# Banded attention with a feed-forward layer: q and k of tile 2 transposed by DMA at one visit of three, score runs joined, one gelu and a table load moved, half of a value load moved

## The chip, the cores and the metric

The kernel runs on one core of one Trainium2 chip. The metric is the time of one execution in device microseconds; the profile shows one execution with its engines TensorE (PE, with its weight loads as PEld), VectorE (DVE), ScalarE (ACT), GpSimd (POOL) and SyncE (SP).

## What is computed

Sliding-window attention over 8 batches of 8 heads, 576 positions, head dimension 64, followed by a two-layer feed-forward over all 4608 tokens of width 512 (hidden width 2048). The reference, cut to what matters:

```python
scores = q @ k.T / sqrt(64)
scores = where(abs(i - j) <= 32, scores, -1e9)
attn   = softmax(scores)
x      = (attn @ v)            # heads side by side: 4608 x 512
h      = x @ w_in
out    = (h * sigmoid(1.702 * h)) @ w_out
```

Inputs and output are float32 in device memory.

## The kernel before, in words

**Units and tiles.** The tokens are cut into 36 *units* of 128 (`NU`) and 9 *tiles* of 512, four units each (`NT`). A unit's attention needs its own 128 keys and the 64 after them. For each unit:

- POOL issues DMAs that load q, k and v with a conversion to bfloat16 (`load_kq`, L137; `load_v`, L208; both together in `fetch`, L802, or by choice in `ahead`, L794). q and k land in staging buffers, five of each (L140). v lands in one of nine tiles `ve`; POOL then copies the odd half-blocks into `vo` (`odd_v`, L218).
- q and k are transposed to `qT` and `kT`, either by DMA from SP's queue (`T_dma`, L236; `turn`, L811, is the pair q u, k u+1) or by TensorE (`T_pe`, L242: four 128x128 transposes for each operand into PSUM, then one copy for each on ACT). Both write a buffer given by `place` (L231).
- `scores` (L267) makes 24 matmuls on 64x64 tiles of the array into two PSUM banks, and two exponentials on ACT that write `p`. `band` (L308) multiplies `p` by the window's mask on VectorE. `values` (L316) makes 32 matmuls on 128x64 tiles, with a column of ones for the softmax sum. `norm` (L335) divides on VectorE. `x_T` and `x_T2` (L385, L400) transpose the result for the feed-forward; in the steady tiles the DMA does it from SP's queue (L393).
- The pairs (0, 1) and (2, 3) run through `scores_pair` (L286), 40 matmuls for two units, since five blocks of 64 keys cover two units together.

**Feed-forward.** Tile 0 runs its first layer plainly (`layer1_plain`, L477), either a 512-column matmul for one ff tile of 128 or, with `half`, two ff tiles of 256 columns each; with `later` the gelu is put on a list and run afterwards, and with `kept` VectorE first copies the result out of PSUM. The other tiles use a seven-product scheme for 2x2 blocks in both layers (`l1_group`, L512; `layer2`, L597), whose sums of weights (`w1_sums`, `w2_sums`), of x (`x_sums`, into `xs`) and of g (`g_sums`, `g0_sum`) VectorE forms. In `l1_group`, products 1, 7, 6, 2, 5, 4, 3 follow each other; VectorE adds into `e` (L537) and into `c` (L543), and ACT runs four gelus (L524). Between the products, `fill` puts in matmuls of the second layer, popped one by one from the list `l2`, and sums for VectorE, from the list `dv`.

**What sets the order.** It is written out by hand: every engine executes its instructions in the order in which the Python code issues them. Each DMA queue (POOL's for loads, SP's for stores and DMA transposes) is in order too: an instruction that waits holds back all behind it. A buffer is taken again when what used it is done.

The parts around the change: `opening` (L662) does the attention of units 0 to 7 and the first layer of tile 0; `first_layer1` (L958) does the first layer of tile 1 in four groups n = 0 to 3, loads q, k and v of units 12 to 16 and turns q and k 8 to 14; `run` (L895) then does the attention of units 8 to 15 between second-layer matmuls and hands over to `back(2)` (L847), the first layer of tile 2, and to the steady loop of `front` and `back`.

In `first_layer1` before, for group n:

```python
if n == 3: self.turn(12); self.turn(13)
self.odd_v(8 + n, gpsimd); self.fetch(12 + n)
... at fill 7 of groups 1, 2, 3:
self.T_pe([("k8","q8","k9"), ("q9","k10","q10"), ("k11","q11","k12")][n - 1], scalar)
```

ACT's gelu and its exponential need different function tables; the first use after the other kind stands behind a table load. A one-element exponential on `spark` (L743) sets the place of the load in the opening.

Of the kernel before, what the change touches and what calls it, by code (L numbers as in the profile page):

```python
# [22 lines left out]
SQ = 64  # L23
# [3 lines left out]
class _Kernel:  # L27
# [180 lines left out]
    def load_v(self, u, which=slice(None)):  # L208
# [3 lines left out]
        for off, b, s, n in list(self.pieces(128 * u, 128))[which]:  # L212
            self.nc.gpsimd.dma_start(t[off:off + n, :, :self.D], self.v[b, :, s:s + n, :].rearrange("h s d -> s h d"))  # L213

    def odd(self, u):
        return self.vo[u % 5 if u < 16 else (2, 3, 4, 0)[u % 4]]
# [49 lines left out]

    def scores(self, u, tag):  # L267
# [15 lines left out]
        for eo in range(2):  # L283
            self.nc.scalar.activation(p[:, eo].rearrange("k h s -> k (h s)"), sc[eo], AF.Exp, scale=self.scale)  # L284

    def scores_pair(self, u):  # L286
# [16 lines left out]
        for x in range(2):  # L303
            for eo in range(2):
                self.nc.scalar.activation(p[:, eo, x].rearrange("k h b s -> k (h b s)"), sc[2 * x + eo], AF.Exp,
                                          scale=self.scale)

    def band(self, u, eng=None):  # L308
# [3 lines left out]
        pv = p.rearrange("p e (h b) s -> p (e h) b s", b=2)  # L312
        msk = self.mask[:, a:b + 1:b - a, :].rearrange("p (o b) s -> p o b s", o=1)
        (eng or self.nc.vector).tensor_mul(pv, pv, msk.to_broadcast([128, 8, 2, SQ]))  # L314
# [39 lines left out]
    def values_four(self, u):  # L354
# [5 lines left out]
        for tag in self.FOUR:  # L360
            lo, n, pad = self.four(tag)
            for i in range(n):
                x, h = divmod(lo + i, self.H)
                at, more = pad + i * (D + 1), pad * (i == 0)
                for blk in range(2):
                    vt = (self.ve[(u + x) % 9], self.odd(u + x))[blk].rearrange("p h d -> p (h d)")
                    self.mm(self.acc[u][tag][64 * blk:64 * blk + 64, at - more:at + D + 1],
                            p[x][:, h % 2, h // 2 * 2 + blk, :], vt[:, h * (D + 2) - more:h * (D + 2) + D + 1],
                            start=(i == 0))
# [199 lines left out]
    def layer2_plain(self, t, pr):  # L569
# [3 lines left out]
        def part(i, f):  # L573
# [88 lines left out]
    def opening(self):  # L662
# [80 lines left out]
        act.activation(self.spark, self.spark, AF.Exp)  # L743
        gelus = []
        kept = [self.sb("s7", [128, 512], F32, 2)]
        room = self.sb("xs", [128, 2, 512], F32, 1, "room")
        kept += [room[:, i, :] for i in range(2)]
        h[:], n[0] = ["LA"], 0
        l1(1, 10, later=gelus, kept=kept[0])
        for i in (3, 1):  # L750
# [8 lines left out]
        self.scores(5, "t")  # L759
        l1(None, 12, later=gelus, kept=kept[1])  # L760
        self.scores(6, "BE")
        self.band(4)
        l1(None, 13, later=gelus, kept=kept[2])
        self.scores(7, "AC")
# [130 lines left out]
    def run(self):  # L895
# [20 lines left out]
        do(more, 4)  # L916
        self.values(8, "t")
# [18 lines left out]
        self.scores(14, "BE")  # L936
        do(more, 4)
        self.x_T(10, "A", dve)
        do(more, 2)
        self.x_T(11, "C", dve)  # L940
        self.scores(15, "t")
        do(more, 2)
        do(self.x_sums(2))
        self.seed2 = dve
        self.odd_v(14, pool)
# [12 lines left out]
    def first_layer1(self):  # L958

        def b(*which):  # L960
            return [lambda i=i, j=j: self.w2_sums((i,), j) for i, j in which]

        dv = b((3, 0), (3, 1), (1, 0), (1, 1))
        extra = {0: [lambda: self.w1_sums((4,), 1), lambda: self.g0_sum(1)] + b((2, 0), (2, 1)), 1: b((4, 0), (4, 1)),
                 2: [lambda: self.g0_sum(2)], 3: []}
        for n in range(4):
            if n == 3:
                self.turn(12)
                self.turn(13)
            self.odd_v(8 + n, self.nc.gpsimd)  # L970
            self.fetch(12 + n)

            def fill(i):
                self.do(self.l2, dict(zip((1, 7, 2, 4), ((1, 1, 3, 3), (1, 1, 3, 5), (2, 2, 8, 4), (2, 2, 6, 6))[n]))[i])
                self.do(dv, {1: 2, 7: 1, 2: 0, 4: 2}[i] if n else {1: 0, 7: 1, 2: 0, 4: 1}[i])
# [3 lines left out]
            self.l1_group(1, n, fill, lambda i: self.do(dv, 1))  # L979
            dv += self.g_sums(1, 2 * n, 2) + extra[n]  # L980
        return dv
# [46 lines left out]
```

## Time and profile before

| What | us |
|---|---|
| three runs, median (lowest to highest) | 279.79 (279.43 to 280.37) |
| the profiled execution | 279.59 |
| its span | 277.8 |
| TensorE busy, of the span | 266.3 |
| VectorE, ACT, POOL busy | 212.1, 197.3, 138.6 |

The profile is a page of summaries and a trace that answers questions. A row of a timeline has the start in us from the span's start, the duration in us, the engine and line, the operation, what it writes `<-` what it reads, the shapes, and in brackets how long the engine had been idle and who released it. Matmuls are pipelined: a matmul's duration is its way through the array, and its slot is the distance to the next start. DMA rows show the issue; the time from issue to landing is a line of its own.

### The profile page before, as it was taken

The page shows a single profiled execution, that of the slowest core. Times are in us where ns is not written, and L with a number is a line of the kernel's source. Part 1 is how long each engine was busy: PE and PEld are TensorE (multiplying, and loading weights), DVE is VectorE, ACT ScalarE, POOL GpSimd, SP SyncE. Part 2 cuts the span into 40 slices and gives each one's busy share as a digit, 9 for nine tenths or more (in the row PEclk, how much of TensorE's full clock was granted, in tenths as well). Part 3 has the DMA queues.
Part 4 walks back from the last instruction along what each step waited for, and adds up shares of the span by engine and source line. Part 5 has one row for each costly group of instructions (what it writes and reads, how often), then busy time and mean ns, then how long its engine had stood idle before and what let it go on. Part 6 is the DMA issues. An engine that isn't in the chain of part 4 may idle for free.

```text
span 277.8 us, 8904 instructions
## 1 busy us (share of the span) xinstructions
PE 266.3 (96%) x3652; PEld 224.8 (81%) x3652; DVE 212.1 (76%) x487; ACT 197.3 (71%) x346; POOL 138.6 (50%) x216
## 2 busy tenths in 40 slices
PE   1989999999999999999999999999999999999994
PEld 1668656888888888888888888888888888888883
DVE  3455898897899788878888887888798878855631
ACT  2586896989896689568966895698569856577420
POOL 8895597999592089729641974294430000000000
PEclk9999999999999999999999999999999999999999
DMA  8999999999999999999999999999992024202033
GB/s 86 166 206 195 178 207 168 170 150 164 139 162 189 155 121 153 174 176 166 188 178 153 130 172 148 163 145 139 136 136 77 2 82 74 76 2 76 2 113 117
DMA packets 150809, 37.74 MB, mean 136 GB/s; under 512 B 138608, under 2 KB 146416, under 8 KB 150768
## 3 DMA queue, kind: packets, MB, share of 16 engines
q0 software_dynamic: 106656, 18.42, 96.4%
q1 hardware_dynamic: 43664, 18.23, 38.0%
q8 instruction: 28, 0.46, 0.7%
q10 hardware_dynamic: 448, 0.52, 0.6%
q14 instruction: 13, 0.11, 0.1%
HBM read 36.83 MB, written 9.44 MB: 167 GB/s over the span
## 4 chain that ended last, share of the span: by engine, by line
PE 91%; DVE 4%; ACT 2%; issue 1%; POOL 1%; POOLq 0%; DVEq 0%
PE o L70 40%; PE h L70 39%; PE sc L70 5%; PE pv L70 4%; PE tp L179 1%; PE tp L203 1%; POOL kq L154 1%; ACT p L284 1%; DVE xn L345 1%; PE tp L409 0%; PE tp L249 0%; DVE b L433 0%; DVE o_sb L67 0%; PE tp L397 0%; ACT kq L67 0%
## 5 line engine op out<-in xcount | busy, mean ns | idle before, releaser
L524 ACT ACTIVATE g<-h 128x512 f16<-128x512 f32 x128 | 72.2, 599 | 37.9 <-PE h L70 31.6
L70 PEld LDWEIGHTS <-g 128*128 128x128 f16 x568 | 54.6, 98 | 8.1
L70 PE MATMUL h<-xs,a 128*128 128x256 f16 x384 | 57.6, 272 | 0.3 <-DVE h L537 0.3
L70 PEld LDWEIGHTS <-a 128*128 128x128 f16 x512 | 49.7, 97 | 8.8 <-issue 0.6
L70 PEld LDWEIGHTS <-w 128*128 128x128 f16 x496 | 47.6, 98 | 7.7
L70 PE MATMUL h<-xT,w 128*128 128x256 f16 (+1 forms) x368 | 53.6, 277 | 0.1
L70 PE MATMUL o<-w,g 128*128 128x256 f16 (+1 forms) x304 | 49.8, 284 | 0.0
L70 PEld LDWEIGHTS <-gs 128*128 128x128 f16 x416 | 39.7, 98 | 5.5 <-issue 0.2
L227 POOL COPY vo<-ve 64x264 int32<-64x264 int32 x71 | 35.1, 494 | 16.4 <-DMA ve<-in_v_dram 10.0
L70 PE MATMUL o<-b,gs 128*128 128x256 f16 x280 | 43.3, 273 | 0.0
L70 PE MATMUL o<-b,g 128*128 128x256 f16 x264 | 38.5, 273 | 0.0
L213 POOL DMA_DIRECT2D ve<-in_v_dram x40 | 34.1, 860 | 5.4 <-DMA w<-in_moe_w_out_dram 1.8
L537 DVE TENSOR_TENSOR h<-h,s 128x512 f32<-128x512 f32 x32 | 22.3, 698 | 18.3 <-PE h L70 18.2
L284 ACT ACTIVATE p<-sc 128x512 bf16<-128x512 f32 x64 | 32.6, 619 | 1.1 <-PE sc L70 1.0
L143 POOL DMA_DIRECT2D qst<-in_q_dram x35 | 28.2, 807 | 1.7 <-issue 1.6
L543 DVE TENSOR_TENSOR h<-h,s 128x512 f32<-128x512 f32 x32 | 22.3, 698 | 7.6 <-PE h L70 7.4
L143 POOL DMA_DIRECT2D kst<-in_k_dram x31 | 26.4, 854 | 0.6 <-DMA qst<-in_q_dram 0.4
L67 ACT COPY h<-h 128x512 f32<-128x512 f32 x32 | 18.8, 589 | 10.4 <-PE h L70 9.8
L886 POOL COPY seen<-gs 1x1 f16<-1x1 f16 x17 | 3.3, 196 | 39.3 <-DVE gs L456 39.3
L314 DVE TENSOR_TENSOR p<-p,mask 128x1024 bf16<-128x1024 bf16 x32 | 21.8, 699 | 0.7 <-ACT p L284 0.7
L67 ACT COPY o_sb<-o 128x256 f32<-128x256 f32 (+1 forms) x24 | 11.1, 462 | 12.8 <-PE o L70 12.8
L67 ACT COPY s<-h 128x512 f32<-128x512 f32 x32 | 19.2, 600 | 0.8
(94 smaller groups left out, 377.8 us busy)
## 6 DMA issues: line engine op xcount, KB each, us to landing
out_dram<-o_sb SPq DMA_DIRECT2D x33, 256.0 KB, 3.8
ve<-in_v_dram POOLq DMA_DIRECT2D x32, 128.0 KB, 6.3
kst<-in_k_dram POOLq DMA_DIRECT2D x25, 128.0 KB, 6.0
qst<-in_q_dram POOLq DMA_DIRECT2D x21, 128.0 KB, 5.7
w<-in_moe_w_out_dram POOLq DMA_DIRECT2D x4, 512.0 KB, 11.1
w<-in_moe_w_in_dram POOLq DMA_DIRECT2D x3, 512.0 KB, 9.3
qst<-in_q_dram POOLq DMA_DIRECT2D x7, 96.0 KB, 6.0
kq<-in_q_dram POOLq DMA_DIRECT2D x2, 256.0 KB, 6.0
```

What stands on the lines that cost most here:

```text
L67: (eng.copy if eng is self.nc.scalar else eng.tensor_copy)(out, in_)
L70: self.nc.tensor.matmul(out, lhsT, rhs, start=start, stop=stop, skip_group_check=True)
L143: self.nc.gpsimd.dma_start(t[off:off + n], src[b, :, s:s + n, :].rearrange("h s d -> s h d"))
L154: self.nc.gpsimd.dma_start(self.stage["first"][0:n // j, :, at:at + j], src[0, :, lo:lo + n, :].rearrange("h (p j) d -> p h j d", j=j))
L213: self.nc.gpsimd.dma_start(t[off:off + n, :, :self.D], self.v[b, :, s:s + n, :].rearrange("h s d -> s h d"))
L227: eng.tensor_copy(*((words(vo[64:128]), words(self.ve[u % 9][64:128])), (words(vo[0:64]), words(nxt)))[i])
L284: self.nc.scalar.activation(p[:, eo].rearrange("k h s -> k (h s)"), sc[eo], AF.Exp, scale=self.scale)
L314: (eng or self.nc.vector).tensor_mul(pv, pv, msk.to_broadcast([128, 8, 2, SQ]))
L524: act.activation(g[:, f, 256 * half:256 * half + 256], bank.rearrange("p (i n) -> p i n", i=2), AF.Gelu_apprx_sigmoid)
L537: dve.tensor_add(e, b, s7)
L543: dve.tensor_add(c, b, s7)
L886: self.nc.gpsimd.tensor_copy(self.seen, self.gs[t - (n == 0)][0:1, 2, c, 255:256])
```

## The change

It touches the opening, tile 1's first layer and the attention of units 8 to 15:

1. **Third visit by transfers.** k 11, q 11 and k 12, which TensorE transposed in group 3, are transposed by DMA from SP's queue, issued at the start of group 1. q 12, k 13, q 13 and k 14 stay with SP in group 3. The loads of v 13 to v 16, which followed each pair of q and k, come together after k 16.
2. **Joined runs.** `scores_two` makes the scores of units 8 and 9, and of 12 and 13, with 40 matmuls; q of such a pair shares one buffer `q_two`. The scores of unit 10 follow those of 8 and 9 directly, with one of their two exponentials held back (`hold`) until later. Values 10 follow scores 12 and 13 directly. Second-layer matmuls are cut into other chunks: six more in tile 1's groups, six fewer after them.
3. **Opening.** ff tiles 8 to 11 are made whole (512 columns) instead of in halves. Tile 10's gelu joins the list that runs behind the exponentials, `kept` gets a fourth place, and the exponentials' table load stands ahead of the transposes of q. The copy of x 4 and 5 goes to VectorE.
4. **Copies.** The two plain second-layer output copies that VectorE made go to ACT, as do those of unit 8 to 15's stretch; x 10 and x 11 are transposed together.
5. **Half of values 8 behind w_out.** v of unit 8 is loaded in two halves of 64 rows, one before and one after w_out's four loads.

The diff, cut to its core:

```diff
+    def load_half(self, u, at):
+        b, s = divmod(128 * u + at, self.S)
+        self.nc.gpsimd.dma_start(self.ve[u % 9][at:at + 64, :, :self.D],
+                                 self.v[b, :, s:s + 64, :].rearrange("h s d -> s h d"))
...
     def place(self, c, u):
+        if c == "q" and u in (8, 9, 12, 13):
+            if u % 2 == 0:
+                self.qT[u] = self.sb("q_two", [128, 4, 256], BF16, 2)
+            return self.qT[u - u % 2][:, :, 128 * (u % 2):128 * (u % 2) + 128]
...
+    def scores_two(self, u, tags):
+        k, q = [self.kT[u + i] for i in range(3)], self.qT[u]
+        sc = [x for tag in tags for x in self.score_banks(tag)]
+        for hp in range(4):
+            c = 256 * (hp % 2)
+            for eo in range(2):
+                r = slice(64 * eo, 64 * eo + 64)
+                for i in range(5):
+                    lo, hi = max(0, 64 * (i - 1)), min(256, 64 * (i + 1))
+                    rows = slice(64 * (i % 2), 64 * (i % 2) + 64)
+                    self.mm(sc[2 * (hp // 2) + eo][rows, c + lo:c + hi], k[i // 2][r, hp, rows], q[r, hp, lo:hi],
+                            start=c == 0 and i < 2)
...
-                self.copy((self.nc.vector, self.nc.scalar)[i * pr], st["o"][:, i, :], st[i])
+                self.copy(self.nc.scalar, st["o"][:, i, :], st[i])
...
-        for u in (5, 6, 7, 8):
+        for u in (5, 6, 7):
             self.load_v(u)
+        self.load_half(8, 0)
         for c in range(4):
             self.load_w2(c)
+        self.load_half(8, 64)
...
-        l1(0, 8)
+        l1(None, 8)
         self.T_four("k", "BE", (dve, act))
...
-        l1(0, 10)
-        l1(1, 8)
+        l1(None, 9)
+        l1(None, 10, later=gelus, kept=kept[0])
+        act.activation(self.spark, self.spark, AF.Exp)
         self.T_four("q", "tA", (dve, act))
-        act.activation(self.spark, self.spark, AF.Exp)
-        l1(1, 10, later=gelus, kept=kept[0])
+        l1(None, 11, later=gelus, kept=kept[1])
...
+        self.x_T2(4, "A", dve)
         self.w1_sums((2,), 1)
         self.g0_sum(0)
-        self.x_T2(4, "A", act)
...
@@ def run(self):
-        self.scores(8, "t")
-        self.scores(9, "AC")
+        do(more, 3)
+        self.scores_two(8, ("t", "AC"))
+        exps = self.scores(10, "BE", True)
         self.turn(14)
         self.turn(15)
         do(late)
-        do(more, 20)
-        self.scores(10, "BE")
-        do(more, 12)
-        self.l2eng = dve
+        do(more, 3)
         self.band(8)
         self.band(9)
-        do(more, 4)
+        self.l2eng = act
+        do(more, 16)
+        do(exps)
+        do(more, 8)
         self.values(8, "t")
         self.values(9, "AC")
...
-        do(more, 8)
-        self.scores(12, "t")
-        do(more, 4)
+        do(more, 12)
+        self.scores_two(12, ("t", "BE"))
         self.values(10, "AC")
+        self.band(11)
         self.norm(10)
-        self.band(11)
-        self.scores(13, "BE")
...
@@ def first_layer1(self):
-            if n == 3:
-                self.turn(12)
-                self.turn(13)
+            for x in ((), ("k11", "q11", "k12"), (), ("q12", "k13", "q13", "k14"))[n]:
+                self.T_dma(x[0], int(x[1:]))
             self.odd_v(8 + n, self.nc.gpsimd)
-            self.fetch(12 + n)
+            self.ahead("kq", 12 + n)
+            for u in ((), (), (), (13, 14, 15, 16))[n]:
+                self.load_v(u)
+            chunks = ((1, 2, 3, 3), (2, 2, 5, 4), (4, 4, 5, 4), (4, 4, 5, 4))[n]
+            sums = ((0, 0, 1, 1, 2), (2, 1, 1, 1, 2), (2, 1, 1, 1, 1), (2, 1, 1, 1, 1))[n]
...
-                if i == 7 and n:
-                    self.T_pe([("k8", "q8", "k9"), ("q9", "k10", "q10"), ("k11", "q11", "k12")][n - 1], self.nc.scalar)
+                if i == 7 and n in (1, 2):
+                    self.T_pe((("k8", "q8", "k9"), ("q9", "k10", "q10"))[n - 1], self.nc.scalar)
```

More of the change, by code (lines that the diff above doesn't have):

```diff
@@ L265, in seed, with scores @@
             self.mm(x, self.ident, self.bias, start=True)
-    def scores(self, u, tag):
+    def scores(self, u, tag, hold=False):
         kT, q = self.kT[u], self.qT[u]
@@ L282, in scores @@
         p = self.p[u] = self.pp[:, u % 2]
-        for eo in range(2):
-            self.nc.scalar.activation(p[:, eo].rearrange("k h s -> k (h s)"), sc[eo], AF.Exp, scale=self.scale)
+        exps = [lambda eo=eo: self.nc.scalar.activation(p[:, eo].rearrange("k h s -> k (h s)"), sc[eo], AF.Exp,
+                                                         scale=self.scale) for eo in range(2)]
+        self.do(exps, 1 if hold else 2)
+        return exps
     def scores_pair(self, u):
@@ L306, in scores_pair @@
                                           scale=self.scale)
+    def scores_two(self, u, tags):
[10 more added lines that the diff above has]
+                            start=c == 0 and i < 2)
+        self.pp = self.sb("p", [128, 2, 2, 8, SQ], BF16, 2)
+        p = self.pp.rearrange("k e x (y b) s -> k e x y b s", y=2)
+        for i in range(2):
+            self.p[u + i] = p[:, :, :, :, 2 * i:2 * i + 2, :]
+        for x in range(2):
+            for eo in range(2):
+                self.nc.scalar.activation(p[:, eo, x].rearrange("k y b s -> k (y b s)"), sc[2 * x + eo], AF.Exp,
+                                          scale=self.scale)
     def band(self, u, eng=None):
@@ L739, in opening @@
         self.g0_sum(7)
-        l1(0, 10)
-        l1(1, 8)
-        self.T_four("q", "tA", (dve, act))
[L743 to L747, printed above, removed]
+        l1(None, 9)
+        gelus = []
+        room = self.sb("xs", [128, 2, 512], F32, 1, "room")
+        kept = [self.sb("s7", [128, 512], F32, 2) for i in range(2)] + [room[:, i, :] for i in range(2)]
+        l1(None, 10, later=gelus, kept=kept[0])
+        act.activation(self.spark, self.spark, AF.Exp)
+        self.T_four("q", "tA", (dve, act))
         h[:], n[0] = ["LA"], 0
-        l1(1, 10, later=gelus, kept=kept[0])
+        l1(None, 11, later=gelus, kept=kept[1])
         for i in (3, 1):
@@ L759, in opening @@
         self.scores(5, "t")
-        l1(None, 12, later=gelus, kept=kept[1])
+        l1(None, 12, later=gelus, kept=kept[2])
         self.scores(6, "BE")
         self.band(4)
-        l1(None, 13, later=gelus, kept=kept[2])
+        l1(None, 13, later=gelus, kept=kept[3])
         self.scores(7, "AC")
@@ L936, in run @@
         self.scores(14, "BE")
[L937 to L940, printed above, removed]
+        do(more, 6)
+        self.x_T2(10, "A", dve)
         self.scores(15, "t")
@@ L943, in run @@
         do(self.x_sums(2))
-        self.seed2 = dve
+        self.seed2 = self.l2eng = dve
         self.odd_v(14, pool)
```

15 lines of the change are left out of this document (9 added, 6 removed).

## The prediction, made before the changed kernel had run

> **What bounds the kernel now.** The page first: busy time, then the chain of work that ended last.
>
> ```profile
> span 277.8 us, 8904 instructions
> PE 266.3 (96%) x3652; PEld 224.8 (81%) x3652; DVE 212.1 (76%) x487; ACT 197.3 (71%) x346; POOL 138.6 (50%) x216
> ...
> PE 91%; DVE 4%; ACT 2%; issue 1%; POOL 1%; POOLq 0%; DVEq 0%
> ```
>
> TensorE is busy for 96% of the span and makes 91% of the chain. So there are two ways to a gain: fewer matmul slots, or fewer of the short waits left. And one way to a loss: anything that arrives after TensorE wants it, for TensorE works in order and has no slack to win it back. The profiled execution took 279.59 us, 1.79 more than its span; the median of the three runs shown is 279.79, 0.2 above it.
>
> **Slots on TensorE.** The timeline of TensorE, start and duration first, prices them (and one row of VectorE's, below it):
>
> ```profile
> 56.63 1.04 PE L70 MATMUL o<-b,gs 128*128 128x256 f16 x8
> 57.92 0.60 PE L70 MATMUL h<-xs,a 128*128 128x256 f16 x4 [0.25 <-DVE h L537]
> ...
> 61.05 0.39 PE L249 MATMUL tp<-ident,kst 128*128 128x128 bf16 x4
> ...
> 61.72 0.60 PE L70 MATMUL h<-xs,a 128*128 128x256 f16 x4
> 62.16 0.60 PE L70 MATMUL h<-xT,w 128*128 128x256 f16 x4
> ...
> 67.40 1.04 PE L70 MATMUL o<-w,g 128*128 128x256 f16 x8
> 68.37 0.45 PE L70 MATMUL sc<-qT,kT 64*64 64x64 bf16 x24
> 68.74 1.05 PE L70 MATMUL o<-w,gs 128*128 128x256 f16 x8
> ```
> ```profile
> 53.74 0.68 DVE L67 COPY o_sb<-o 128x512 f32<-128x512 f32 x1
> ```
>
> Starts, not durations, give a slot: four matmuls of 256 columns take 0.44 (61.72 to 62.16), 0.11 each.
>
> - *Third visit.* Its twelve transposes fill 61.05 to 61.72: **-0.67**. They become three DMA transposes on SP's queue, and three copies on ACT go, both off the path here.
> - *Joined runs.* Eight second-layer matmuls should take 0.87, but from 67.40 to 68.37 are 0.97: a change from 128-row tiles to 64-row tiles costs 0.10, and I take as much for the way back, so the 24 score matmuls themselves take 0.27 of the 0.37 before 68.74. Scores 10 now stand behind scores 8 and 9, scores 13 beside 12, values 10 straight behind them: four changes fewer, **-0.40**. A joined pair takes 40 matmuls for 48, at 0.011 each: 16 fewer, **-0.18**.
> - *Stall at 57.92.* Eight matmuls from 56.63 end at 57.51, so 0.41 is lost waiting for VectorE's addition into `e`. Two 128x512 output copies, the second at 53.74, leave VectorE for ACT just ahead of it (0.68 each), and the three ACT copies that vanish make up for them there: **-0.41**.
> - Whole tiles of layer 1 in place of halves keep their columns (16 matmuls of 512 for 32 of 256): 0. Second-layer chunks only change places: 0.
>
> **Opening.** ACT's timeline, then TensorE's:
>
> ```profile
> 28.78 0.60 ACT L495 ACTIVATE g<-h 128x512 f16<-128x512 f32 x1
> ...
> 30.69 1.01 ACT L67 COPY kq<-tp 128x1024 bf16<-128x1024 bf16 x1 [0.45 <-PE tp L203]
> 31.73 1.28 ACT L743 ACT_TABLE_LOAD   x1
> 33.13 4.00 ACT L284 ACTIVATE p<-sc 128x512 bf16<-128x512 f32 x8
> ```
> ```profile
> 34.70 0.45 PE L70 MATMUL sc<-kq 64*64 64x64 bf16 x24
> 35.22 0.19 PE L70 MATMUL pv<-ve,p 128*64 128x65 bf16 x1
> ```
>
> Tile 10's gelu moves behind the exponentials, so the table load stands ahead of the copy instead of behind it. ACT is then free at about 29.4 (28.78 + 0.60), load and spark, 1.40 by the rows 31.73 and 33.13, end at 30.8, and the copy starts 0.1 later than at 30.69: scores 4 wait for it, **+0.1**. The exponentials start 0.8 earlier, so the wait before values 4 (34.70 to 35.22 is 0.52 against 0.37, 0.15) goes: **-0.15**. The sixth gelu fits into those 0.8. The copy of x 4 and 5 goes from ACT (1.01) to VectorE, where it takes the place of waiting for ACT: 0.
>
> The Trainium skill, "ScalarE: Activation LUTs", section "What ACT_TABLE_LOAD costs", gives about 2.66 us for a change of tables, 1.38 of it a drain. Here the exponentials start 1.40 after the load does, with another ACTIVATE between; by the page scores 4 would start some 1.3 later still, which the rows don't bear out.
>
> **Exponentials of 8 to 10.**
>
> ```profile
> 66.19 1.28 ACT L284 ACT_TABLE_LOAD   x1
> 67.49 3.05 ACT L284 ACTIVATE p<-sc 128x512 bf16<-128x512 f32 x6
> ```
> ```profile
> 69.59 0.69 DVE L314 TENSOR_TENSOR p<-p,mask 128x1024 bf16<-128x1024 bf16 x1 [0.29 <-ACT p L284]
> ```
>
> A joined pair needs all four exponentials before its first mask product: from the last gelu of tile 1, 1.3 of load, 3 x 0.49 + 0.6 of exponentials, 0.69 + 0.6 for two masks, 4.7 until values 9 may start. TensorE has 1.0 less to do in this stretch (of the terms above) and runs into it: I take **+0.7** (0.3 to 1.1).
>
> Subtotal where tile 2's layer 1 starts: -0.67 - 0.40 - 0.18 - 0.41 - 0.05 + 0.7 = **-1.0**.
>
> **The transfers.** Here the change adds waits. The loads of k and q have five buffers each. The load of k 13 takes the first of five k buffers that comes free. Before, TensorE's visit frees k 8's; now the DMA transpose of k 11 stands first and frees k 11's, so POOL's queue holds k 13 until that transpose has landed. Behind it in the queue wait the odd copy for 9, q 13 (for q 11's transpose), k 14 (for k 12's), and all that follows. POOL's timeline, SP's, and the landing times of k loads issued from 46 to 68 us, of k transposes from 59 to 93, of x transposes from 93 to 98:
>
> ```profile
> 47.65 0.90 POOL L143 DMA_DIRECT2D kst<-in_k_dram  x1
> ...
> 53.78 1.39 POOL L143 DMA_DIRECT2D kst<-in_k_dram  x2
> 55.13 1.40 POOL L213 DMA_DIRECT2D ve<-in_v_dram  x2
> ...
> 58.81 0.89 POOL L143 DMA_DIRECT2D kst<-in_k_dram  x1
> ...
> 66.47 0.88 POOL L143 DMA_DIRECT2D kst<-in_k_dram  x1 [0.19 <-issue]
> 67.33 0.88 POOL L213 DMA_DIRECT2D ve<-in_v_dram  x1
> ...
> 75.21 0.88 POOL L143 DMA_DIRECT2D qst<-in_q_dram  x1
> ```
> ```profile
> 72.83 1.19 SPq L240 DMA_TRANSPOSE kT<-kst  x1
> ...
> 81.95 1.19 SPq L240 DMA_TRANSPOSE qT<-qst  x1
> ...
> 93.89 5.67 SPq L393 DMA_TRANSPOSE xT<-xn  x4
> ```
> ```profile
> DMA to landing us min/median/max: 5.2/5.4/6.2
> ```
> ```profile
> DMA to landing us min/median/max: 3.6/5.3/6.7
> ```
> ```profile
> DMA to landing us min/median/max: 3.7/3.9/5.9
> ```
>
> Step by step, at the medians: k 11 is issued at 47.65, some 0.3 later with one more transfer ahead (values 8 in halves); lands 53.1; its transpose lands 58.4 (56.7 to 59.8). k 13 goes out at 58.4 instead of 53.78, 4.6 late. From k 13 to k 14 were 5.03; without the 1.40 of v 13 they are 3.6: k 14 at 62.0 instead of 58.81, by when k 12's transpose has landed too (61.5, worked out alike). v 13 to v 16 (1.40 and three of 0.9, 4.1 together) now come behind k 16. From k 14 to k 16, 7.66 without two of 0.9: k 16 at 67.9, 1.4 late. Then v 13 to 16: the last is issued at 72.0 (67.9 + 0.88 + 1.40 + 1.8) instead of 67.33 and lands at about 77.5; the odd copy for 15 needs it, and q 16 stands behind: 77.9 instead of 75.21, **2.7 late**.
>
> What waits for these:
>
> ```profile
> 77.78 0.45 PE L70 MATMUL sc<-qT,kT 64*64 64x64 bf16 x24
> ...
> 78.39 0.60 PE L70 MATMUL h<-xT,w 128*128 128x256 f16 x4
> ...
> 105.34 0.60 PE L70 MATMUL h<-xs,a 128*128 128x256 f16 x4
> ...
> 106.32 0.60 PE L70 MATMUL h<-xs,a 128*128 128x256 f16 x4
> ```
> ```profile
> 104.08 0.42 DVE L441 TENSOR_TENSOR xs<-xT 128x512 f16<-128x512 f16 x1
> ...
> 105.20 0.51 DVE L441 TENSOR_TENSOR xs<-xT,xs 128x512 f16<-128x512 f16 x1
> ```
>
> - *Scores 12 to 15.* k 14 lands at 67.4, its transpose at 72.6; the joined scores 12 want it at about 72.3: 0.4. Scores 15 want k 16: loaded by 73.8, transposed 3.6 to 5.3 later, 77.3 to 79.0; without waits TensorE is there at 77.78 - 1.0 = 76.8. I take 78.3: scores 15 start 0.5 later than before instead of 1.0 sooner, a wait of **+1.5** in all, and layer 1 of tile 2 at 78.9 for 78.39.
> - *x of tile 3.* SP issues everything from 81.95 (q 16) to 99.56 without a gap, the four x transposes last. The last goes out at 97.88 and lands 5.9 later, 103.8; VectorE forms the differences (104.08 to 105.71), TensorE wants them at 105.34 and 106.32. Slack: 106.32 - 103.8 - 1.65, 0.85. With q 16 late by 2.7 (2.2 if it lands faster than the 6.7 of before's), that product starts 1.3 to 1.9 late at a landing of 5.9, and not late at all at 3.9. I take **+1.0**.
>
> The two don't add: TensorE already 0.5 late meets the second with that much less. The later one decides: **+1.0** over the span. After that every tile is as before, and nothing comes back.
>
> Sum: 279.59 + 1.0 = 280.6, and 0.2 for the median: **280.8 us**.
>
> **Rivals.**
> 1. *Transfers land soon, and the gain stays.* For it: landings of 3.6 and 3.7 occur where few loads run, and POOL's wait itself thins them out. Against it: with loads in flight the transposes took 5.3. It decides when k 12's and k 16's transposes both land within about 4.0. Then k 14 goes out at 60.7 and scores 15 wait for nothing: the -1.0 remains up to tile 3, whose x lands no later than 103.5: **278.7**. [...]
> 2. *It cancels.* The x transposes land at 3.9, scores 15 wait 1.0 instead of 1.5: gain and wait balance within 0.5: **279.8**.
> 3. *The chain is longer.* Landings at the upper rows (6.2 and 6.7): k 13 at 59.8 and k 14 near 63.5, q 16 4 late, x of tile 3 3.1 to 3.6 late on the path: **283**.
>
> **Chances.** Forecast (280.0 to 282.2) 0.55; rival 1 0.13; rival 2 0.24; rival 3 0.08. A measurement of this kernel tells 0.3%, 0.84 us, from no change. Above 280.63: 0.42 of the forecast's 0.55 and rival 3, 0.50. Below 278.95: rival 1 but for 0.01, 0.12. Between: 0.38. For 8 in 10 the range takes most of rival 1's edge and part of rival 3: 279.0 to 282.6.
>
> **What would show it.** Right: the transposes at L249 down from 36 to 24; no idle before `h` near 57.9; POOL idle some 4 us before k 13's load, ended by a DMA transpose; idle on TensorE or its weight loads ahead of scores 12, 14 or 15, ended by `qT`, `kT` or `q_two`; VectorE's first `xs` of tile 3 waiting for `xT`; equal lengths of every later tile. Wrong: k 13 loaded by 55, scores 15 before 77, tile 2's layer 1 starting before 78. Wrong in size rather than cause: an x transpose of tile 3 landing before 104.

## The result, and the profile after

The changed kernel takes **283.98 us** (median of five runs, 283.61 to 284.67) against 279.43 for the kernel before on the same chip (279.28 to 280.37): ratio 1.0159, 95% interval 1.0139 to 1.0179, so 4.6 us slower. The forecast was 280.8. Ratios here and below count only executions within 1.5% of the fastest of their kernel; the medians of e7, r10 and r11 below also contain one or two that were slower than that. Its profiled execution took 284.08 us. Line numbers here are those of the changed kernel; `T_dma` is L249 and `T_pe` is L258.

The page of after: the span, TensorE's busy time and the chain that ended last.

```profile
span 282.3 us, 8812 instructions
...
PE 265.5 (94%) x3608; PEld 221.5 (78%) x3608; DVE 211.3 (75%) x485; ACT 195.4 (69%) x345; POOL 138.1 (49%) x217
...
PE 82%; DMA 8%; POOL 3%; ACT 3%; DVE 1%; issue 1%; POOLq 0%; DVEq 0%
```

TensorE has 44 matmuls fewer and is busy 0.8 us less, yet the span grew by 4.5. The chain says where to look: TensorE's share fell from 91% to 82%, and 8% now belong to transfers, which had no place in it: about 2% each to a transpose of k and to one of x, and 3% to a load of weights in the opening, for which TensorE itself waited only 0.47 us. Next, GpSimd's timeline of after (start, duration, and in brackets the idle time ahead and what ended it).

```profile
57.96 1.36 POOL L143 DMA_DIRECT2D kst<-in_k_dram  x2 [4.17 <-DMA kT<-kst]
...
67.03 0.88 POOL L143 DMA_DIRECT2D kst<-in_k_dram  x1
67.89 4.02 POOL L213 DMA_DIRECT2D ve<-in_v_dram  x5
...
79.53 0.40 POOL L232 COPY vo<-ve 64x264 int32<-64x264 int32 x1 [1.86 <-DMA ve<-in_v_dram]
80.35 0.88 POOL L143 DMA_DIRECT2D qst<-in_q_dram  x1 [0.42 <-issue]
```

GpSimd stands idle for 4.17 us ahead of k 13's load (57.96), until k 11's DMA transpose has landed, as forecast, and k 16's load goes out at 67.03. But q 16's load goes out at 80.35, 5.1 late where 2.7 was forecast: the odd copy for 15 had to wait for v 16. TensorE's timeline shows who pays.

```profile
57.61 0.71 PE L70 MATMUL o<-b,gs 128*128 128x256 f16 x5
58.20 0.60 PE L70 MATMUL h<-xs,a 128*128 128x256 f16 x4
...
66.67 1.04 PE L70 MATMUL o<-w,g 128*128 128x256 f16 x8
68.13 1.03 PE L70 MATMUL o<-w,gs 128*128 128x256 f16 x8 [0.43 <-DVE o_sb L658]
...
70.03 0.22 PE L70 MATMUL pv<-ve,p 128*64 128x65 bf16 x1
...
70.63 0.22 PE L70 MATMUL pv<-ve,p 128*64 128x65 bf16 x1 [0.16 <-DVE p L348]
...
75.58 0.24 PE L70 MATMUL sc<-qT,kT 64*64 64x64 bf16 x2
77.17 0.44 PE L70 MATMUL sc<-qT,kT 64*64 64x64 bf16 x22 [1.35 <-DMA kT<-kst]
...
79.75 0.80 PE L70 MATMUL sc<-qT,kT 64*64 64x64 bf16 x24 [0.93 <-DMA qT<-qst]
...
80.71 0.60 PE L70 MATMUL h<-xT,w 128*128 128x256 f16 x4
...
100.32 0.60 PE L70 MATMUL h<-xs,a 128*128 128x256 f16 x4 [0.24 <-DVE h L572]
...
109.25 0.61 PE L70 MATMUL h<-xs,a 128*128 128x256 f16 x4 [1.07 <-DVE xs L476]
```

The stall ahead of `h` at 57.9 is gone (five matmuls of 0.11 take 57.61 to 58.16, `h` starts at 58.20). In its place, from row to row: 0.59 at 68.13 and 0.16 and 0.32 ahead of values 8 and 9 (the exponentials); 1.54 inside scores 14 (75.58 and 77.17), 1.10 ahead of scores 15 (79.75) and 0.30 inside them (transposes of k and q); 1.23 at 109.25 (x of tile 3). Layer 1 of tile 2 starts at 80.71 instead of 78.39, 2.32 late; the product at 109.25 stood at 105.34, 3.91 late. After that the distance stays (last output copy 278.20 for 274.28). The other 0.6 of the span's 4.5 us stand behind that copy: 4.1 us from it to the end instead of 3.5, for which no row shows a cause.

SyncE's queue, VectorE's wait, and the landing times of k transposes issued from 59 to 93 and of x transposes from 97 to 104, the windows of before moved along:

```profile
73.18 1.21 SPq L249 DMA_TRANSPOSE kT<-kst  x1
...
84.09 1.19 SPq L249 DMA_TRANSPOSE qT<-qst  x1
...
89.08 1.19 SPq L249 DMA_TRANSPOSE kT<-kst  x1
...
97.61 5.73 SPq L428 DMA_TRANSPOSE xT<-xn  x4
```
```profile
108.76 0.42 DVE L476 TENSOR_TENSOR xs<-xT 128x512 f16<-128x512 f16 x1 [1.92 <-DMA xT<-xn]
```
```profile
DMA to landing us min/median/max: 4.0/6.4/7.6
```
```profile
DMA to landing us min/median/max: 4.9/5.9/7.2
```

The medians went from 5.3 to 6.4 and from 3.9 to 5.9: the transposes got slower. A row of the page of before that the prediction did not use bears on why, the share of the DMA engines' time that is busy, in 40 slices:

```profile
DMA  8999999999999999999999999999992024202033
```

For the first 208 us, but for the first slice, the engines are 90% busy or more. A transfer added there could take its time from those behind it. The row alone does not show that it does: s2 below tests it.

### The profile page after: what moved, and what is told of

Read it like the earlier page. It is cut to its first block, busy times and chain, and to the rows that moved or that the text cites. A ratio compares the mean times of both kernels' runs of the same rounds, so it can differ in the third digit from the quotient of the medians.

```text
span 282.3 us, 8812 instructions
## 1 busy us (share of the span) xinstructions
PE 265.5 (94%) x3608; PEld 221.5 (78%) x3608; DVE 211.3 (75%) x485; ACT 195.4 (69%) x345; POOL 138.1 (49%) x217
## 4 chain that ended last, share of the span: by engine, by line
PE 82%; DMA 8%; POOL 3%; ACT 3%; DVE 1%; issue 1%; POOLq 0%; DVEq 0%
PE h L70 39%; PE o L70 36%; DMA w<-in_moe_w_in_dram 3%; PE pv L70 3%; PE sc L70 3%; DMA kT<-kst 2%; DMA xT<-xn 2%; POOL ve L213 1%; POOL kq L154 1%; ACT p L338 1%; ACT kq L67 1%; ACT g L559 1%; POOL w L127 1%; PE tp L258 0%; DVE p L348 0%
## 5 line engine op out<-in xcount | busy, mean ns | idle before, releaser
L70 PEld LDWEIGHTS <-w 128*128 128x128 f16 x480 | 45.9, 98 | 9.2 <-DMA w<-in_moe_w_in_dram 0.6
L232 POOL COPY vo<-ve 64x264 int32<-64x264 int32 x71 | 34.1, 480 | 22.0 <-DMA ve<-in_v_dram 18.7
L213 POOL DMA_DIRECT2D ve<-in_v_dram x39 | 33.2, 866 | 2.8 <-DMA w<-in_moe_w_in_dram 1.6
L292 ACT ACTIVATE p<-sc 128x512 bf16<-128x512 f32 x56 | 28.7, 624 | 3.8 <-PE sc L70 3.7
L67 ACT COPY o_sb<-o 128x256 f32<-128x256 f32 (+1 forms) x27 | 12.7, 470 | 12.6 <-PE o L70 12.6
```

The costliest lines, as they stand in the source:

```text
L67: (eng.copy if eng is self.nc.scalar else eng.tensor_copy)(out, in_)
L70: self.nc.tensor.matmul(out, lhsT, rhs, start=start, stop=stop, skip_group_check=True)
L232: eng.tensor_copy(*((words(vo[64:128]), words(self.ve[u % 9][64:128])), (words(vo[0:64]), words(nxt)))[i])
L292: exps = [lambda eo=eo: self.nc.scalar.activation(p[:, eo].rearrange("k h s -> k (h s)"), sc[eo], AF.Exp, scale=self.scale) for eo in rang ...
```

## The experiments

Each time is a median beside the kernel before on the same chip, which gave 279.3 to 279.5 throughout. **Theory A**: holding GpSimd's queue for k 11's transpose is the loss. **Theory B**: the v loads put behind k 16 are. **C, E, F**: the rest of the change costs more than read. **G**: three more DMA transposes are the loss as traffic. Staging buffers are the tiles `kst` and `qst`, five each.

### Each move undone

**e1_v_between**: the v loads back.

```
-            self.ahead("kq", 12 + n)
-            for u in ((), (), (), (13, 14, 15, 16))[n]:
-                self.load_v(u)
+            self.fetch(12 + n)
```

> The changed kernel with the loads of v 13 to 16 put back between those of k and q; the third visit stays with the transfers. Theory A (the queue of GpSimd is held until k 11's DMA transpose has landed, so all that is behind k 13 is late): k 13 still goes out at about 58, k 16 goes out 2 to 3 us later than at 67.0, the wait ahead of scores 14 and 15 (2.9 us after the change) stays or grows, 283 to 285 us. Theory B (the four v loads behind k 16 slow the last transposes and hold q 16): k 16's transpose lands in 4 to 5.5 us instead of 6.9, q 16 goes out near 77 instead of 80.35, the wait ahead of x of tile 3 (1.2) goes, 281 to 282.5 us.

Measured 285.35 us, ratio 1.0207 (1.0183 to 1.0231). This is just over the end of A's range, and B is out as the sole cause. With the queue held, putting v behind k 16 did no harm: k 16 goes out at 67.03 in the changed kernel and at 71.47 in e1. Whether it gained something is open, since TensorE's clock fell in e1 (last section), which is worth more than the 1.4 us between the two.

**e2_visit_on_pe**: the third visit back on TensorE, v still last.

```
-            for x in ((), ("k11", "q11", "k12"), (), ("q12", "k13", "q13", "k14"))[n]:
+            for x in ((), (), (), ("q12", "k13", "q13", "k14"))[n]:
-                if i == 7 and n in (1, 2):
-                    self.T_pe((("k8", "q8", "k9"), ("q9", "k10", "q10"))[n - 1], self.nc.scalar)
+                if i == 7 and n:
+                    self.T_pe((("k8", "q8", "k9"), ("q9", "k10", "q10"), ("k11", "q11", "k12"))[n - 1], self.nc.scalar)
```

> The changed kernel with the third visit (k 11, q 11, k 12) back on TensorE; v 13 to 16 still behind k 16. Theory A: k 13 goes out near 53.8, k 16 near 64, the waits ahead of scores 14 and 15 and ahead of x of tile 3 (2.9 and 1.6) go, 0.65 comes back for the transposes: 280.1 us (279.6 to 280.7). Theory B: the last transposes still land in 6.5 to 8 us and q 16 waits for v 16, a wait of over 1 us stays at one of the two places: 281.5 to 283.

Measured 284.6 us, 1.0167 (1.0139 to 1.0195): a miss for A and worse than B's range. GpSimd's timeline tells why:

```profile
58.59 0.90 POOL L143 DMA_DIRECT2D kst<-in_k_dram  x1
...
64.47 0.88 POOL L143 DMA_DIRECT2D qst<-in_q_dram  x1 [4.07 <-DMA q_two<-qst]
```

One hold is gone and another there: q 14's load now takes the buffer that q 12's DMA transpose frees. The kernel's code does not say so; it follows from which buffer came free first. So this run undid less than it seemed to (s3 below).

**e3_visit_on_pe_v_between**: both of these edits.

> The changed kernel with both undone: third visit on TensorE, v loads between those of k and q. What is left of the change is the joined runs, the opening, the copies on ScalarE and the halves of values 8. A and B both: no wait ahead of scores 14, 15 and x of tile 3, as in the kernel before; by the trace of after the rest is worth -0.1 to -0.5 against it: 279.0 to 279.9 us. Theory C (the joined runs cost more than the traces of the transfers show): 280.5 or more.

Measured 281.12 us, 1.0056 (1.0038 to 1.0074), which is theory C: what is left of the change costs 1.7 us where the sum had a gain of 0.3.

**e4_seven_k_buffers**: the changed kernel, seven buffers for k and six for q.

```
-        t = self.stage[c, u] = self.sb(c + "st", [128, self.H, self.D], BF16, 5)
+        t = self.stage[c, u] = self.sb(c + "st", [128, self.H, self.D], BF16, 7 if c == "k" else 6)
```

> The changed kernel with seven staging buffers for k and six for q in place of five each, so that k 13 and k 14 need not wait for any transpose; all transfers and their order as in the change. Theory A: k 13 goes out near 53.8, the waits of 2.9 and 1.6 go almost wholly: 279.3 to 280.3 us. Theory B: the v loads stay behind k 16 and in its transposes' way: a wait of 1 to 2 us ahead of scores 15 or of x of tile 3 stays, 281 to 283 us.

Measured 281.34 us, 1.0084 (1.0053 to 1.0115). The hold is worth 2.6 of the 4.6 by the medians and 2.1 by the ratios. What is left fits B's range, but e3 has shown 1.7 of it to be the other edits.

### The third visit alone

**e7_before_visit_by_transfers**: the kernel before with one edit.

```
+            if n == 1:
+                for x in ("k11", "q11", "k12"):
+                    self.T_dma(x[0], int(x[1:]))
-                if i == 7 and n:
+                if i == 7 and n in (1, 2):
```

> The kernel BEFORE with one edit: k 11, q 11 and k 12 by DMA transposes issued ahead of group 1 of tile 1, the third visit of TensorE gone; everything else as before. Theory A (holding GpSimd's queue for k 11's transpose is enough by itself): k 13's load at 57 to 59 instead of 53.8, waits of 2 to 4 us ahead of scores 12 to 15, 282 to 284 us. Rival D (it does harm only beside the other parts, with the moved v loads or the joined pairs' buffers): 278.8 to 280.

Measured **284.25 us**, 1.0166 (1.0132 to 1.0199): as much as the whole change. That is the upper end of A's range, and rival D is out. GpSimd, then TensorE:

```profile
60.29 1.36 POOL L143 DMA_DIRECT2D kst<-in_k_dram  x2 [5.93 <-DMA kT<-kst]
```
```profile
75.79 0.24 PE L70 MATMUL sc<-qT,kT 64*64 64x64 bf16 x2 [1.99 <-DMA qT<-qst]
77.86 0.64 PE L70 MATMUL sc<-qT,kT 64*64 64x64 bf16 x22 [1.83 <-DMA kT<-kst]
78.43 1.04 PE L70 MATMUL o<-w,g 128*128 128x256 f16 x4
79.26 1.06 PE L70 MATMUL o<-b,g 128*128 128x256 f16 x4
```

**r9_visit_seven_buffers**: e7 with seven buffers each (`BF16, 7)` in the line shown at e4). **s1_before_seven_buffers**: the kernel before with these buffers alone.

> The kernel BEFORE with the third visit by transfers (as in e7_before_visit_by_transfers, 284.25 us) and seven staging buffers each for k and q in place of five, so that k 13 and k 14 wait for no transpose. Theory A (all of e7's loss is the hold of GpSimd's queue behind k 11's transpose): k 13 goes out near 53.8, no wait over 0.3 us ahead of scores 12 to 15, and the 0.65 us of the twelve transposes stay saved: 278.6 to 279.0 us. Rival G (three more DMA transposes on SyncE's queue are the loss, held loads or not): 282 us or more.

> The kernel BEFORE with seven staging buffers each for k and q, and nothing else: the control for r9_visit_seven_buffers. Both theories: nothing holds these loads in the kernel before, so 279.2 to 279.6 us. Were it 280 or more, the buffers themselves (loads that start sooner) would be part of what r9 lost.

s1: 279.34 us, 0.9998 (0.9988 to 1.0007), so the buffers alone change nothing. r9: 280.46 us, 1.0035 (1.0021 to 1.0049). By the ratios e7 loses 4.6 us and r9 1.0, so about 3.6 of e7's loss are the hold. But by theory A r9 should have gained 0.65, and it lost 1.0, a miss of 1.6. Its TensorE waits for k 15's transpose, though no load was held (k 13 at 53.80):

```profile
53.80 1.39 POOL L143 DMA_DIRECT2D kst<-in_k_dram  x2
```
```profile
77.52 0.44 PE L70 MATMUL sc<-qT,kT 64*64 64x64 bf16 x22 [1.08 <-DMA kT<-kst]
```

**s2_three_idle_transposes**: s1 with the three DMA transposes as mere traffic. TensorE makes its visit as before; the results of the three are read by nobody.

```
+            if n == 1:
+                for c, u in (("k", 11), ("q", 11), ("k", 12)):
+                    self.nc.sync.dma_start_transpose(self.sb("idle", [128, 4, 128], BF16, 3),
+                                                     self.stage[c, u].rearrange("p h d -> p (h d)"))
```

> s1_before_seven_buffers with three DMA transposes more, of k 11, q 11 and k 12 into a scratch tile that nobody reads, ahead of group 1 of tile 1; TensorE still makes its third visit. They add traffic and places on SyncE's queue and take nothing away. Theory G (r9 lost 1.7 us net of its 0.65 because the DMA engines have no room there: the loads behind land 2 us later): 280.7 to 281.4 us, q 15's load landing 7 us or more after its issue. Rival (the loss in r9 was the use of the transposes, for which values or scores wait): 279.2 to 279.8.

Measured 280.67 us, 1.0039 (1.0027 to 1.0052): just under G's range, and 1.3 more than s1 by the medians (1.1 by the ratios) for transfers that no one waits for. GpSimd issues its loads when s1 does up to v 16's (67.00 and 67.04), and SyncE q 12's and k 13's transposes too (58.73 and 60.07 for 58.74 and 60.16), so neither queue is held by the three; what comes later is the landing. The landing times of the three k transposes issued from 58 to 70, of s1, s2 and r9 in turn:

```profile
DMA to landing us min/median/max: 5.2/6.0/6.4
```
```profile
DMA to landing us min/median/max: 6.8/7.2/7.6
```
```profile
DMA to landing us min/median/max: 6.7/7.5/8.2
```

TensorE pays in s2 where it paid in after, 0.24 us inside scores 14 and then at x of tile 3:

```profile
106.50 0.61 PE L70 MATMUL h<-xs,a 128*128 128x256 f16 x4 [0.61 <-DVE xs L441]
```

G is right for the part that A leaves: three transfers more made those behind land 1.2 to 1.5 us later. So the third visit by transfers costs about 3.6 for the hold and some 1.1 to 1.6 for traffic, and saves 0.65.

### The v loads

**r11_before_v_last**: the kernel before, v 13 to 16 behind k 16 (e1's edit the other way round). **s3_e2_seven_buffers**: e2 with seven buffers for k and six for q.

> The kernel BEFORE with one edit: v 13 to 16 loaded behind k 16 in place of between; third visit on TensorE. Theory B (four v loads in a row behind k 16 slow the last two transposes, and q 16 waits through the odd copy for v 16): q 16 goes out near 80 instead of 75.2, waits of 1 to 1.8 us ahead of scores 15 and 1 to 2 ahead of x of tile 3, 282 to 283.5 us. Rival (the order of the loads matters only where the queue is held): 279 to 280.

> e2_visit_on_pe (third visit on TensorE, v 13 to 16 behind k 16, all else as changed; 284.6 us) with seven staging buffers for k and six for q. In e2's trace GpSimd stood 4.1 us ahead of q 14's load, for a staging buffer that q 12's DMA transpose frees. Theory A' (a held load is the loss there too, only another one): the hold goes, 281 to 282.2 us, what the remaining edits (1.7) and the v order (0.9) cost one by one. Rival B (the v loads behind k 16 are the loss by themselves, beside the joined pairs): 283.5 or more.

r11: 280.25 us, 1.0036 (1.0011 to 1.0060); just over the rival's range; q 16 went out at 76.17, not near 80, so B's steps did not come about. s3: 281.94 us, 1.0091 (1.0065 to 1.0116), as A' has it; q 14's load goes out 4.5 earlier than in e2:

```profile
59.98 0.88 POOL L143 DMA_DIRECT2D qst<-in_q_dram  x1
```

By itself the move of the v loads costs 0.9 (r11 over the kernel before) to 1.6 (s3 over s5, below). In e2 over e3 it is 3.5, since there it also lengthens the hold ahead of q 14's load, from 1.73 us in e3's trace to 4.07.

### The other edits

**e5_e3_old_opening**: e3 with the opening of the kernel before. **r12_before_values8_halves**: the kernel before with the halves alone:

```
-        for u in (5, 6, 7, 8):
+        for u in (5, 6, 7):
             self.load_v(u)
+        self.load_half(8, 0)
         for c in range(4):
             self.load_w2(c)
+        self.load_half(8, 64)
```

> The changed kernel with the third visit on TensorE and the v loads between (as in e3_visit_on_pe_v_between, 281.1 us), and with the whole opening of the kernel before: values 8 in one load ahead of w_out, tile 10's gelu and the table load in their old places. Theory E (the second half of values 8 waits for a place among the eight transfers in flight and pushes the odd copies 4 to 7 back, so values 4 and 5 wait some 0.4 and 0.3 us, while the table's earlier load gains nothing): 0.4 to 0.6 us less than e3, 280.5 to 280.7, no wait inside values 4 and 5. Rival: the opening is worth nothing either way, 281.1.

> The kernel BEFORE with one edit: values 8 loaded in two halves, the second behind w_out. Theory E (the ninth transfer waits for a place, the odd copies 4 to 7 start some 0.8 us later, values 4 and 5 wait for them): 0.3 to 0.6 us more, 279.7 to 280.0, with a wait inside values 4 ended by a vo copy. Rival (as forecast, the second half is hidden): 279.4.

e5: 280.21 us, 1.0047 (1.0028 to 1.0067), the median 0.9 under e3's, but the ratio only by 0.0009, and the intervals overlap. r12: 279.55, 1.0004 (0.9990 to 1.0018): the halves alone cost nothing that can be told, against E. E's chain begins in r12's trace too, where the odd copies start at 33.91 instead of 33.05, but values 4 do not wait for them there; in e3's trace they do, GpSimd first, then TensorE in values 4:

```profile
33.28 0.69 POOL L217 DMA_DIRECT2D ve<-in_v_dram  x1 [0.79 <-DMA ve<-in_v_dram]
34.02 4.97 POOL L232 COPY vo<-ve 64x264 int32<-64x264 int32 x8
```
```profile
35.34 0.19 PE L70 MATMUL pv<-vo,p 128*64 128x65 bf16 x1 [0.24 <-POOL vo L232]
```

**e6_e3_scores_8_9_apart**: e3 with scores 8, 9 and 10 as in the kernel before.

```
-        self.scores_two(8, ("t", "AC"))
-        exps = self.scores(10, "BE", True)
+        self.scores(8, "t")
+        self.scores(9, "AC")
...
+        do(more, 14)
+        self.scores(10, "BE")
+        do(more, 12)
```

> e3_visit_on_pe_v_between with scores 8 and 9 as two runs and scores 10 behind 14 second-layer chunks, as in the kernel before; scores 12 and 13 stay joined. Theory F (a joined pair holds its first mask product until all four exponentials are done, and TensorE runs into that: 1.4 us in e3's trace at the second layer, values 8 and values 9): the three waits go, 0.3 comes back for two changes of form and eight matmuls, 280.0 to 280.4 us. Rival (the waits are the transfers' doing, or move on to the next place): 281 or more.

Measured 280.98 us, 1.0056 (1.0035 to 1.0078): no gain. e3's trace had waits of 0.35, 0.26 and 0.36 there:

```profile
68.91 1.03 PE L70 MATMUL o<-w,gs 128*128 128x256 f16 x8 [0.35 <-DVE o_sb L658]
...
71.08 0.22 PE L70 MATMUL pv<-ve,p 128*64 128x65 bf16 x1 [0.26 <-ACT o_sb L67]
...
71.88 0.22 PE L70 MATMUL pv<-ve,p 128*64 128x65 bf16 x1 [0.36 <-DVE p L348]
```

In e6's trace they are down to one of 0.26, and the profiled execution, 279.92, is next to the shortest of eight (279.81 to 282.56). F's waits go, but the median does not follow.

**s5_e3_seven_buffers**: e3 with seven and six buffers. **t1_e3_old_opening_and_8_9**: e5 and e6 in one.

> e3_visit_on_pe_v_between (third visit on TensorE, v loads between, all else as changed; 281.1 us) with seven staging buffers for k and six for q. Theory A' (in e3's trace GpSimd stood 1.7 us ahead of q 14's load for q 12's DMA transpose, and k 16's transpose landed 1.7 us later than in the kernel before): the hold and a wait of 0.3 us inside scores 15 go, 280.3 to 280.8 us. Rival: the 1.7 us that e3 is over the kernel before lie wholly on TensorE and its helpers (exponentials, values 4 and 5): 281 or more.

> e3_visit_on_pe_v_between with both the old opening (e5) and scores 8 and 9 apart (e6). What stays of the change is scores 12 and 13 joined, the copies on ScalarE and the new shares of second-layer products in tile 1. If opening and joined pair are the 1.7 us and each hid the other when undone alone: 279.3 to 279.9 us. If the new shares and the held load of q 14 are: 280.3 or more.

s5: 280.34 us, 1.0031 (1.0017 to 1.0045), as A' had it: 0.8 under e3, though the intervals overlap. t1: 280.61, 1.0048 (1.0022 to 1.0074), 0.5 under e3; in its trace GpSimd stands 0.27 us ahead of q 14's load instead of 1.73, so there this hold was gone as well. How the 1.7 us divide among the edits is therefore not settled. s5's trace shows where most of its own rest is lost. One part is a wait for VectorE in the first layer of tile 2:

```profile
98.10 0.60 PE L70 MATMUL h<-xs,a 128*128 128x256 f16 x4 [0.23 <-DVE h L572]
```

The row ahead of it starts 0.95 us earlier, where the kernel before takes 0.59 (97.06 to 97.65), so 0.36 are lost. This wait stands in the traces of after and of all seven variants with its opening, and in none with the old opening; why VectorE comes later there, no row says. The other part stands behind the last output copy: 4.0 us to the end for 3.5, as in after.

### Looking for a version that beats both

**e8_before_copies_joined_12**: the kernel before with what looked free: both 512-column copies on ScalarE, scores 12 and 13 joined.

```
-                self.copy((self.nc.vector, self.nc.scalar)[i * pr], st["o"][:, i, :], st[i])
+                self.copy(self.nc.scalar, st["o"][:, i, :], st[i])
...
-        self.scores(12, "t")
+        do(more, 4)
+        self.scores_two(12, ("t", "BE"))
...
-        self.scores(13, "BE")
```

> The kernel BEFORE with two edits: both 512-column output copies of tile 0 on ScalarE, and scores 12 and 13 joined; nothing else. From the terms that the traces bear out (0.42 for the stall ahead of h at 57.9, 0.3 for two changes of form and eight matmuls): 278.6 to 278.9 us. Rival (the joined pair 12/13 holds values 12's masks as 8/9 does, or ScalarE is late with its copies of the third visit): 279.4 or more.

**s4_e8_seven_buffers** is e8 with seven buffers each, **r10_best_of_all** is s4 with the third visit by transfers.

> e8_before_copies_joined_12 (third visit on TensorE, output copies of tile 0 on ScalarE, scores 12 and 13 joined; 279.26 us, its profiled execution 278.66) with seven staging buffers each for k and q. If e8's spread came from held loads: 278.6 to 278.9 us and a narrower spread, below the kernel before. If not: 279.1 to 279.4 again.

> r9_visit_seven_buffers with both 512-column output copies of tile 0 on ScalarE and scores 12 and 13 joined (the two edits of e8_before_copies_joined_12): with ScalarE rid of the three copies of the third visit. Theory A and the traces' terms (0.65, 0.42, 0.3): 278.0 to 278.5 us. Rival G: as r9, 282 or more. Rival (the run-to-run spread of the transfers takes the gains, as in e8): within 0.3 of the kernel before.

e8: 279.26 us, 1.0001 (0.9985 to 1.0016). Its profiled execution has a span of 276.9, 0.9 under the kernel before, but it is the second shortest of twelve (278.58 to 280.64). s4: 279.46, 0.9996 (0.9983 to 1.0009). r10: 281.4, 1.0062 (1.0039 to 1.0086), no better than r9. So none of the three is told apart from the kernel before on the faster side. That 0.9 us fewer in one profile are none in the median shows how little one execution can carry.

## Why the prediction was right in direction and wrong in size

- **The hold** (right). k 13 waits for k 11's transpose: forecast 58.4, came 57.96; k 16 67.9 and 67.03. Shown by e4 (2.1 to 2.6 us less) and by r9 against e7 (about 3.6 less).
- **"x of tile 3 ... I take +1.0"** (mis-sized; the step that failed, since this term is the whole of the sum). It came to 3.91, by this chain. q 16's load went out 5.1 late and not 2.7, since v 16's load landed 8.4 after its issue, not 5.5; the last two v loads of GpSimd's row at 67.89:

```profile
DMA to landing us min/median/max: 6.6/7.5/8.4
```

  q 16's load then landed in 3.7 instead of 6.7, so its transpose was only 2.14 late (84.09 for 81.95). SyncE next stood 1.0 for k 18's load (89.08 for 85.91), and the last x transpose went out at 102.07 for 97.88, 4.19 late, and landed after 6.6 instead of 5.9:

```profile
DMA to landing us min/median/max: 6.6/6.6/6.6
```

  That is 4.9 late, and less the slack of 0.85 it is 4.0.
- **"They become three DMA transposes on SP's queue, and three copies on ACT go, both off the path here"** (wrong; a term put at nothing). The sum had nothing for them but the hold. s2 shows 1.1 to 1.3 us for them as traffic, about twice the 0.65 that leaves TensorE, and the longer landings above fit this, though no run shows that they come from these three alone.
- **Scores 12 to 15, +1.5** (mis-sized). 2.94 us were lost (1.54 + 1.10 + 0.30). The sum took 3.6 to 5.3 for k 16's transpose; the one issued at 73.18 landed after 6.9, at 80.06 instead of 78.3:

```profile
DMA to landing us min/median/max: 6.9/6.9/6.9
```

- **"The two don't add ... The later one decides"** (right). TensorE was 2.32 late at tile 2's layer 1, lost 0.36 more in the wait for VectorE at 100.32, and met x of tile 3 that much late; it paid only the difference there, 1.23.
- **Exponentials, +0.7 (0.3 to 1.1)**: 1.07 in after's trace (0.59 + 0.16 + 0.32), at the upper end. What they cost in the median is open: e6 did not show it.
- **Stall at 57.92, −0.41; twelve transposes, −0.67; joined runs, −0.58; opening, −0.05**: their sum fits the trace. With the exponentials at 1.07 they make −0.64, and at scores 14, where the first wait for a transpose came, the changed kernel was 0.61 ahead (75.58 for the 76.19 below, of the kernel before). Single terms are not measured by that: e8 leaves open whether stall and joined runs bring anything in the median, r12 finds the halves free, and e5 does not settle the rest of the opening.

```profile
76.19 0.45 PE L70 MATMUL sc<-qT,kT 64*64 64x64 bf16 x24
```

- Rival 3, "the chain is longer", at 283 with 0.08, was the nearest: its landings (6.2 and 6.7) and its delay of x (3.1 to 3.6) were near those that came.

## What to carry to other kernels

Before work is moved from an engine to transfers, read the DMA share for that stretch: here, at 90% or more, three transfers more cost 1.1 to 1.3 us although nobody waited for them. Since the share does not say how much, add the transfers as mere traffic, as s2 does, and measure. Then ask which buffer the next load will take and who frees it, since one load held in an in-order queue holds all behind it. And where two late arrivals meet one engine, the later one decides; so it is the later one whose chain has to be sized with care, at the landing times of a fuller queue and not at those of before.

## What the runs showed of the hardware beyond that

**How soon a transfer lands depends on what else is in flight.** In e2, while GpSimd stood for 4 us and issued no loads, the two k transposes issued from 60 to 65 landed in

```profile
DMA to landing us min/median/max: 2.4/2.8/3.2
```

and the same transfer took up to 8.2 in r9. In the kernel before, the last four x transposes (227.9 to 232.0), where the page's row shows 2 to 4 tenths, landed in

```profile
DMA to landing us min/median/max: 2.4/2.5/3.6
```

The row is a coarse guide, though: e2's page shows nines from 60 to 65 as well. The Trainium skill, "DMA: Bandwidth & Descriptors", section "Anatomy of one DMA — SWDGE (gpsimd) path", gives 2.0 us plus bytes at 436 GB/s for transfers that GpSimd issues, an estimate of 2.3 for 128 KB. The rows here don't bear it out under load: such loads took from 3.5 (q 14's in e2, the first after the stand) to 8.4 (v 16's in after).

**TensorE's clock fell after a wait.** In e7, after the two waits of 1.99 and 1.83 us, four matmuls of 256 columns took 0.83 (78.43 to 79.26) instead of 0.44. The stretches of e7 (time; busy time of PE, PEld, DVE, ACT, POOL; then the granted clock):

```profile
73.60:75.80 2.20, 0.21 (x10) 0.10 (x8) 1.85 (x6) 0.30 (x1) 2.03 (x4) 1.00 2.34 156
75.80:78.10 2.30, 0.47 (x17) 0.33 (x20) 0.00 (x0) 0.00 (x0) 1.61 (x4) 0.93 2.88 112
78.10:81.00 2.90, 2.90 (x38) 2.25 (x28) 0.42 (x1) 1.09 (x2) 0.40 (x1) 0.50 1.64 168
81.00:84.00 3.00, 3.00 (x85) 2.50 (x84) 2.32 (x8) 2.39 (x4) 2.83 (x4) 0.97 0.66 149
```

What the last three stretches fall short of a clock of 1.00 makes an estimate of 1.7 us on top of the waits, or 3.4 us at half speed. The same stands in e1's trace behind a wait of 1.85 (0.56 for 3.9 us, again 1.7 and 3.4); in after, behind 1.35 and 0.93, the clock stayed at 1.00. So a wait of about 2 us cost more than its length there. In e7 five of the six executions have a mean granted clock of 0.988 to 0.993; the sixth, at 1.000, is the shortest (282.68). So what e7 loses to the hold contains this as well. The Trainium skill, "TensorE: Matmul & The Clock Gate", section "Part 1: The HAM clock gate (the "warmup" mystery)", has the clock halved after an idle window of about 3.4 us and full again after a busy one of as much. The rows agree on the half and, by the estimates of 3.4, on the length of the recovery; the idle time ahead of it was shorter in e1 than that window.

**Some variants spread more than the kernel before, and the clock is a part of it.** The kernel before stays within 2.3 us in 35 runs (278.87 to 281.13), t1 within 3.6 in twelve (279.16 to 282.77). t1's three longest, 282.44 and more, are the ones with a mean granted clock of 0.993; the other nine have 0.997 or more. e4 spreads over 4.0 (280.12 to 284.12) with hardly any difference in the clock, and r9, which waits for a transpose too, over only 1.3 (279.81 to 281.09). What else makes a kernel spread is not shown.
